# Hash attention and SwiGLU on one core: q and k columns ordered by chunk parity, and an opening laid out anew

## The chip, the core and the metric

The kernel runs on one core of a Trainium2 chip. A core has five engines, each with its own instruction queue: TensorE (PE: matmuls and transposes into PSUM), VectorE (DVE), ScalarE (ACT), GpSimd (POOL) and SyncE (SP, which here only issues DMAs). DMAs can be issued from the queues of SP, ACT and POOL. An engine works through its queue in order; a semaphore holds an instruction until its inputs are there, and everything behind it on that engine waits too. The metric is the device time of one execution in microseconds (us).

## The reference

Attention over 4 batches, 8 heads, 768 tokens of 64 dimensions, followed by a gated feed-forward layer. A query sees only those keys that fall in its bucket; the bucket is the sign pattern of six projections.

```python
q_bits = (np.einsum('bhsd,dk->bhsk', q, proj) > 0)      # and k_bits; proj is 64 x 6
mask = q_bucket[:, :, :, None] == k_bucket[:, :, None, :]
scores = np.where(mask, scale * np.matmul(q, k.transpose(0, 1, 3, 2)), -1000000000.0)
attn = exp(scores - max);  attn = attn / (attn.sum(-1) + 1e-09)
x = (attn @ v) as [batch * seq, heads * head_dim]       # 3072 x 512
xn = x / sqrt(mean(x * x) + 1e-06) * rms_g
g = xn @ w_gate;  out = (g * sigmoid(g) * (xn @ w_val)) @ w_out
```

The gate and value weights are 512 x 1536, the output weights 1536 x 512. Everything comes and goes as float32.

## The kernel before

**The mask as rows of a matmul.** A score tile is one matmul over 71 rows: 64 rows hold the scaled dimensions of q and k (factor `DIM`), six rows hold the bits as +0.5 or -0.5, and one row is a constant. Where all six bits agree the exponent stays at its size; where one differs it is so small that the exponential is nothing. So a pair of heads needs, in one tile `qk` (128 x 4 x 768 fp16: q of two heads, k of two heads), the scaled dimensions in rows 0 to 63, the bits in rows 64 to 69 and the constants.

**Units and slots.** A batch has two units of 384 queries (`hf` 0 and 1), eight units in all. A unit's attention has 24 slots (8 heads x 3 blocks of keys). A slot is two score matmuls (`scores`, L292) of 128 keys x 384 queries, two exponentials on ACT (L299), and later six matmuls with v (`pv`, L322), which add to one PSUM tile for six slots; after those six, `post` normalizes the head pair on DVE (L337, L338). A unit ends with sums of squares (L351), a power on POOL (`rs`, L379), a scaling of x (L386), and transposes of x (L399). Its 12 gate steps (`queue_gates`, L438 to L464) and six output steps (`queue_out`, L488) run in the slots of the next unit and the one after. Thus from the second unit on, TensorE has attention, gates and outputs side by side. In the first unit there is attention alone.

**Preparation of a head pair** (`queue_prep`). Loads put 6 consecutive tokens on each partition, so a chunk of 128 columns is "every sixth token". Four groups of three float32 transposes (L175) turn q and k of two heads; a transpose takes two chunks at once, the even chunk landing in partitions 0 to 63, the odd one in 64 to 127. ACT copies q out of PSUM (`qT`), DVE copies k (`kT`). Eight matmuls (`project`, L186) make the six projections of both parities in one PSUM tile. DVE turns them into bits (L198), and eight DMAs carry these into rows 64 to 69 of `qk`, one for each of q and k of two heads and each parity (`place`, L205). DVE scales the dimensions (`dims`, L238). POOL casts v to fp16 (`vcast`, L243) and adds it up (`vsum`, L251 to L254); the first product of a head pair (L309) needs that sum.

**Parities.** In `qk` the columns stand in the order of the chunks, even and odd in turn. A score matmul's 384 queries are three chunks of both parities. So the first slot of a head waits for the bits and dimensions of both.

**Order.** The code puts every step at a position with `at(pos, fn)`, in units of slots; the list is sorted by it at the end and issued. Unit u's slot n stands at 24u + n. Nothing but the position decides the order within an engine's queue; no step waits for its position in time.

**The opening.** Pair 0 of batch 0 is prepared ahead of slot 0 with two projections, one per parity, from which DVE writes the bits straight into `qk` (`bits_direct`, L221), and ACT does the scaling (L236). Pairs 1, 2 and 3 go through DMAs: pair 1's transposes ahead of slot 0 and its projection after slot 1, pair 2 from position 3.6, pair 3 from 8.6. All gate and value weights are loaded from POOL's queue, casting to fp16, at position 2.0 (`load_gv`, L149), after POOL's casts and sums of v; the output weights follow (L153). Score tiles of the first unit use four buffers of the pool `ring` and three of `gvpool`.

Of the kernel before, what the change touches and what calls it, by code (L numbers as in the profile page):

```python
# [33 lines left out]
def kernel(  # L34
# [47 lines left out]


    warm = const.tile([128, 1], FP32, name="warm")
    nc.vector.memset(warm, 0.0)
    nc.scalar.activation(warm, warm, AF.Exp)
    ident = const.tile([128, 128], FP32, name="ident")
    make_identity(nc, ident)
    pj = const.tile([128, 32], FP32, name="pj")
    nc.vector.memset(pj, 0.0)  # L90
    nc.sync.dma_start(out=pj[0:64, 0:6], in_=proj)
    nc.sync.dma_start(out=pj[64:128, 6:12], in_=proj)
    pj1 = []
    for e in range(2):
        t = const.tile([128, 32], FP32, name=f"pj1_{e}")
        nc.vector.memset(t, 0.0)
        nc.vector.tensor_copy(
            t[64 * e : 64 * e + 64, 0:6], pj[64 * e : 64 * e + 64, 6 * e : 6 * e + 6]
        )
        pj1.append(t)  # L100
    load_v(0, 0)
    for hp in range(1, 4):
        load_qk(0, hp)
        load_v(0, hp)
    grow = const.tile([128, DMODEL], FP32, name="grow")
    nc.sync.dma_start(out=grow, in_=moe_rms_g.unsqueeze(0).partition_broadcast(128))

    NQK = 6
# [10 lines left out]

    def const_rows(i):  # L120
        nc.gpsimd.memset(qks[i][64:71, 0:2, :].bitcast(FP32), ONE_ONE)
        nc.gpsimd.memset(qks[i][64:71, 2:4, :].bitcast(FP32), M15_M15)

    const_rows(0)
    vsums = []
    for i in range(2):
# [3 lines left out]
        vsums.append(t)  # L130
    const_rows(1)
    for i in range(2, NQK):
        at((-11.0, -5.0, 20.0, 21.0)[i - 2], lambda i=i: const_rows(i))

# [23 lines left out]

    def queue_prep(b, hp, p0, step, vp, hlag=0.0, direct=False):
        idx = prep_n[0]  # L160
        prep_n[0] += 1
        qk = qks[idx % NQK]
        qk_of[(b, hp)] = qk
        tl = {}

        def tr(j):
            def go():
                if j == 0:
                    tl["q"] = work.tile([128, 2, HQ], FP32, name="qT", tag="qT")
                    tl["k"] = work.tile([128, 2, HQ], FP32, name="kT", tag="kT")  # L170
                src = loads[(b, hp)][j % 2]
                m = ring.tile([128, 3, 128], FP32, name="trps", tag="r")
                src = src[:, j // 2].rearrange("p (c e) d -> p c (e d)", e=2)
                for i in range(3):
                    nc.tensor.transpose(m[:, i, :], src[:, i, :], ident)  # L175
                dst = tl["qk"[j % 2]][:, j // 2, :]
                mm = m.rearrange("p c d -> p (c d)")
                if j % 2 == 0:
                    nc.scalar.activation(dst, mm, AF.Copy)  # L179
                else:  # L180
                    nc.vector.tensor_copy(dst, mm)  # L181
            return go

        def project(lhs, m):
            for c in range(4):
                nc.tensor.matmul(  # L186
                    m[32 * c : 32 * c + 32, :], lhs, tl["qqkk"[c]][:, c % 2, :],
                    start=True, stop=True, tile_position=(0, 32 * c),
                )

        def parity(ap, e):
            return ap.rearrange("p (c e t) -> p c e t", e=2, t=128)[:, :, e, :]

        def hash_():
            m = ring.tile([128, HQ], FP32, name="hps", tag="r")
            project(pj, m)
            bits = work.tile([128, HQ], FP16, name="bits", tag="bits")
            nc.vector.tensor_scalar(bits, m, 0.0, 0.5, op0=ALU.is_gt, op1=ALU.subtract)  # L198
            tl["bits"] = bits

        def place(c):
            def go():
                for e in range(2):
                    eng = nc.gpsimd if b == 0 and hp == 1 and e else nc.sync
                    eng.dma_start(  # L205
                        out=parity(qk[64:70, c], e),
                        in_=tl["bits"][32 * c + 6 * e : 32 * c + 6 * e + 6, :].rearrange(
                            "p (c t) -> p c t", t=128
                        ),
                    )  # L210
            return go

        def hash_direct():
            tl["ms"] = [ring.tile([128, HQ], FP32, name="hps", tag="r") for _ in range(2)]
            for e in range(2):
                project(pj1[e], tl["ms"][e])

        def bits_direct(c):
            def go():
                for e in range(2):  # L220
                    nc.vector.tensor_scalar(  # L221
                        parity(qk[64:70, c], e),
                        tl["ms"][e][32 * c : 32 * c + 6, :].rearrange("p (c t) -> p c t", t=128),
                        0.0, 0.5, op0=ALU.is_gt, op1=ALU.subtract,
                    )
            return go

        def dims(i):
            def go():
                c, e = i // 2, i % 2  # L230
                dst = qk[0:64, 2 * c : 2 * c + 2].rearrange(
                    "p h (c e t) -> p h c e t", e=2, t=128
                )[:, :, :, e, :]
                src = tl["qk"[c]][64 * e : 64 * e + 64].rearrange("p h (c t) -> p h c t", t=128)
                if direct:
                    nc.scalar.activation(dst, src, AF.Copy, scale=DIM)  # L236
                else:
                    nc.vector.tensor_scalar_mul(dst, src, DIM)  # L238
            return go

        def vcast():
            vl = vloads[(b, hp)]
            nc.gpsimd.tensor_copy(  # L243
                v16s[b % 2][:, :, 2 * hp : 2 * hp + 2, 0:64],
                vl.rearrange("p h c d -> p c h d"),
            )

        def vsum():
            vl = vloads[(b, hp)]
            t3 = work.tile([128, 2, 3, D], FP32, name="vt3", tag="vt3", bufs=1)  # L250
            nc.gpsimd.tensor_add(t3, vl[:, :, 0:3, :], vl[:, :, 3:6, :])  # L251
            t1 = work.tile([128, 2, D], FP32, name="vt1", tag="vt1", bufs=1)
            nc.gpsimd.tensor_add(t1, t3[:, :, 0, :], t3[:, :, 1, :])
            nc.gpsimd.tensor_add(vsums[b % 2][:, hp, 0, :, 0:64], t1, t3[:, :, 2, :])  # L254

        at(vp, vcast)
        at(vp + 0.01, vsum)
        for j in range(4):
            at(p0 + step * j, tr(j))
        if direct:  # L260
            at(p0 + step * 4, hash_direct)
            for i, c in enumerate((0, 2)):
                at(p0 + step * 4 + 0.001 * (i + 1), bits_direct(c))
            for i, c in enumerate((1, 3)):
                at(-1.0 + 0.001 * i, bits_direct(c))
        else:
            at(p0 + step * 4 + hlag, hash_)
            for i, c in enumerate((0, 2, 1, 3)):
                at(p0 + step * 4 + hlag + 0.001 * (i + 1), place(c))
        for i in range(4):  # L270
            at(p0 + step * (4.2 + 0.3 * i) + hlag, dims(i))

# [7 lines left out]
    def queue_attention(u, base, step, late):  # L280
# [22 lines left out]
        def pv(n):  # L303
            def go():
# [13 lines left out]
                for i in range(2):  # L318
                    jt = 2 * blk + i
                    p = probs_of.pop((u, n, i))  # L320
                    for t in range(3):
                        nc.tensor.matmul(  # L322
                            acc[:, t, hh, :],
                            p[:, 128 * t : 128 * t + 128],
                            v16s[b % 2][:, jt, h, :],
                            start=False, stop=(n % 6 == 5 and i == 1 and t == 2),
# [146 lines left out]
    def queue_out(u, pos, last=False):  # L473
# [6 lines left out]
        def outq(j):  # L480
            def go():
# [10 lines left out]
                if half == 1:  # L492
                    dst = out[b * S : (b + 1) * S].rearrange("(p c) m -> p c m", c=6)
                    if last and t == 1:
# [3 lines left out]
                    if last:  # L498
                        nc.sync.dma_start(out=dst[:, 3 * hf + t, :], in_=tl["o"][:, t, :])
                    elif t == 2:  # L500
                        at_later.append(
                            lambda: nc.sync.dma_start(
                                out=dst[:, 3 * hf : 3 * hf + 3, :], in_=tl["o"]
                            )
# [9 lines left out]


    queue_prep(0, 0, -24.0, 1.0, -24.0, direct=True)
    queue_prep(0, 1, -18.0, 1.0, -16.0, hlag=15.2)
    queue_prep(0, 2, 3.6, 1.0, 1.5)
    queue_prep(0, 3, 8.6, 1.0, 1.6)


    for c in range(4):
        for wh in range(2):
            at(2.0 + 0.1 * (2 * c + wh), lambda c=c, wh=wh: load_gv(c, wh))
    for c in range(4):
        at(16.0 + 2.0 * c, lambda c=c: load_wo(c))

# [11 lines left out]
    for u in range(NU):  # L539
        queue_attention(u, SLOTS * u, 1.0, 1.1 if u == 0 else 0.0)  # L540
        p = SLOTS * (u + 1) + 0.6
        if u == 0:
            queue_norm(u, p, 1.0, 3.6)
        else:
            queue_norm(u, p, 1.0, 4.1)
    F = SLOTS / 18.0
    steps = lambda base, js: [base + 0.15 + F * j for j in js]
    for u in range(NU):
        base = SLOTS * (u + 1)
        if u == 0:  # L550
            queue_gates(u, [base + 6.15 + 1.47 * j for j in range(12)], 1.47)
        else:
# [37 lines left out]
```

## Time and profile before

| | |
|---|---|
| median of 3 runs | 393.58 us (390.21 to 394.15) |
| profiled execution | 394.13 us, span 392.4 us |
| mean granted TensorE clock | 0.955 |
| PE busy | 356.6 us, 91% |
| PE weight loads | 214.9 us, 55% |
| ACT busy | 243.4 us, 62% |
| DVE busy | 237.7 us, 61% |
| POOL busy | 77.2 us, 20% |
| instructions | 7949 |

The costliest groups: exponentials on ACT, 384 of 491 ns; score matmuls, 384 of 346 ns; gate and value matmuls, 384 each of 325 and 326 ns; products with v, 1152 of 199 ns; output matmuls, 288 of 379 ns. A duration is from an instruction's start to its end; matmuls overlap, so a row of them takes less than its sum.

In the preparation, over the whole kernel: a copy out of PSUM 552 ns on DVE (L181) and 496 on ACT (L179); a bit write or bit step 551 to 557 ns on DVE; a scaling 64 x 768 about 650 ns mean on DVE (0.540 to 1.260 us) and 843 ns on ACT; a cast of v on POOL 872 ns; its three sums 1115, 567 and 530 ns; a constant fill of seven rows on POOL 731 or 869 ns. Of 120 bit DMAs of 4.5 KB, 116 are issued from SP, at 0.72 us each, and four from POOL, where they land after 1.9, 2.8 and 3.3 us (least, median, most).

How to read it: the busy shares are means over the whole time. The opening, some 60 us, differs from the rest, and what a step there costs has to be read from its own stretch. The granted clock is what share of full speed TensorE's clock had. It is shown as full from the start, but matmuls before about 9 us last as long as those at half clock later (eight projections of 128 x 384: 0.86 us each group at 7.05 as at 23.2, and 0.52 at 14.5).

### The profile page before, as it was taken

How to read it: one execution, taken by the hardware profiler on the slowest of the kernel's cores; microseconds unless marked ns; L12 is line 12 of the kernel's file. 1: busy time of each engine (PE TensorE's matmuls, PEld its weight loads, DVE VectorE, ACT ScalarE, POOL GpSimd, SP SyncE). 2: the span in 40 equal slices, each digit the busy share in tenths (PEclk: the TensorE clock that was granted, in tenths of full speed). 3: DMA queues.
4: the chain of work that ended last, by engine and by line, in shares of the span. 5: the costliest groups of instructions: out<-in, count | busy, mean ns of one | idle time of the engine just before them, and what ended most of it. 6: DMA issues, size and time to landing. Idle time of an engine off the chain costs nothing.

```text
span 392.4 us, 7949 instructions
## 1 busy us (share of the span) xinstructions
PE 356.6 (91%) x3048; PEld 214.9 (55%) x3048; DVE 237.7 (61%) x469; ACT 243.4 (62%) x549; POOL 77.2 (20%) x110
## 2 busy tenths in 40 slices
PE   5765979989999998999999998999999999998995
PEld 3442536656565664656565664656565655563552
DVE  2854164765866678475866668465866564366570
ACT  5753655657676764757676774767675767772321
POOL 6898036020000037200000028200000000000000
PEclk9986557999999999999999999999999999999999
DMA  7729992120000840410000840310000200200102
GB/s 249 263 30 202 223 293 109 43 87 3 3 3 5 297 147 5 147 60 2 2 3 5 295 150 5 132 75 2 3 4 4 83 0 2 82 1 2 81 2 80
DMA packets 23574, 31.22 MB, mean 80 GB/s; under 512 B 4184, under 2 KB 22128, under 8 KB 23536
## 3 DMA queue, kind: packets, MB, share of 16 engines
q1 hardware_dynamic: 17584, 25.97, 19.4%
q0 software_dynamic: 5952, 4.74, 7.9%
q8 instruction: 24, 0.39, 0.4%
q14 instruction: 14, 0.11, 0.1%
HBM read 28.58 MB, written 6.29 MB: 89 GB/s over the span
## 4 chain that ended last, share of the span: by engine, by line
PE 51%; issue 24%; DVE 14%; POOL 5%; DMA 3%; ACT 1%; SPq 1%; POOLq 0%; DVEq 0%; ACTq 0%
PE v_ps L438 11%; PE g_ps L438 10%; PE s_ps L292 9%; PE o_ps L488 9%; PE pv L322 6%; DVE qk L238 4%; DVE xn L386 2%; DVE sq L351 2%; PE trps L175 2%; PE hps L186 2%; DMA vl<-in_v_dram 2%; DMA qk<-bits 2%; DVE x L338 1%; DVE a L455 1%; POOL rs L379 1%
## 5 line engine op out<-in xcount | busy, mean ns | idle before, releaser
L299 ACT ACTIVATE p<-s_ps 128x384 f16<-128x384 f32 x384 | 164.2, 491 | 82.1 <-PE s_ps L292 80.8
L292 PE MATMUL s_ps<-qk 71*128 71x384 f16 x384 | 101.6, 346 | 7.1 <-DMA qk<-bits 5.2
L438 PE MATMUL v_ps<-xnT,wv 128*128 128x384 f16 x384 | 78.1, 326 | 5.9 <-DVE a L455 5.9
L438 PE MATMUL g_ps<-xnT,wg 128*128 128x384 f16 x384 | 79.0, 325 | 4.1 <-ACT xnT L407 2.5
L455 DVE SCALAR_TENSOR_TENSOR a<-th,g_ps 128x384 f32<-128x384 f32 x96 | 53.1, 553 | 46.4 <-ACT th L447 45.2
L322 PEld LDWEIGHTS <-p 128*128 128x128 f16 x1152 | 63.1, 101 | 31.1 <-issue 13.4
L322 PE MATMUL pv<-v,p 128*128 128x65 f16 x1152 | 70.0, 199 | 0.0
L488 PE MATMUL o_ps<-wo,ht 128*128 128x512 f16 x288 | 68.7, 379 | 0.0
L447 ACT ACTIVATE th<-g_ps 128x384 f32<-128x384 f32 x96 | 47.8, 498 | 20.9 <-PE g_ps L438 18.0
L464 DVE TENSOR_TENSOR ht<-a,v_ps 128x384 f16<-128x384 f32 x96 | 53.0, 552 | 8.0
L379 POOL TENSOR_TENSOR rs<-ms,mhalf 128x3 f32<-128x3 f32 x8 | 6.9, 858 | 246.8 <-DVE ms L375 246.8
L438 PEld LDWEIGHTS <-wv 128*128 128x128 f16 x384 | 37.5, 98 | 32.5 <-issue 8.2
L438 PEld LDWEIGHTS <-wg 128*128 128x128 f16 x384 | 35.2, 97 | 26.0 <-issue 6.3
L488 PEld LDWEIGHTS <-ht 128*128 128x128 f16 x288 | 27.0, 97 | 27.4
L292 PEld LDWEIGHTS <-qk 71*128 71x128 f16 x384 | 29.4, 102 | 14.4 <-issue 7.4
L497 ACT ACTIVATE osb<-o_ps 128x512 f32<-128x512 f32 x23 | 13.7, 597 | 24.8 <-PE o_ps L488 24.8
L181 DVE COPY kT<-trps 128x384 f32<-128x384 f32 x32 | 17.7, 552 | 17.2 <-PE trps L175 17.2
L337 DVE RECIPROCAL r<-pv 128x6 f32<-128x6 f32 x32 | 6.2, 193 | 34.9 <-PE pv L322 34.9
L179 ACT ACTIVATE qT<-trps 128x384 f32<-128x384 f32 x32 | 15.9, 496 | 13.9 <-PE trps L175 13.9
L386 DVE SCALAR_TENSOR_TENSOR xn<-x,rs,grow 128x512 f16<-128x512 f32 x24 | 21.1, 932 | 5.6 <-POOL rs L379 5.6
L198 DVE TENSOR_SCALAR bits<-hps 128x384 f16<-128x384 f32 x15 | 8.4, 557 | 21.6 <-PE hps L186 20.9
L175 PE MATMUL trps<-ident,ql 128*128 128x128 f32 x96 | 17.0, 288 | 3.9 <-DMA ql<-in_q_dram 3.9
(50 smaller groups left out, 284.1 us busy)
## 6 DMA issues: line engine op xcount, KB each, us to landing
ql<-in_q_dram SPq DMA_DIRECT2D x16, 384.0 KB
kl<-in_k_dram SPq DMA_DIRECT2D x16, 384.0 KB
vl<-in_v_dram SPq DMA_DIRECT2D x16, 384.0 KB
out_dram<-osb SPq DMA_DIRECT2D x7, 768.0 KB
qk<-bits SPq DMA_DIRECT2D x116, 4.5 KB
wg<-in_moe_w_gate_dram POOLq DMA_DIRECT2D x4, 384.0 KB, 9.0
wv<-in_moe_w_val_dram POOLq DMA_DIRECT2D x4, 384.0 KB, 10.5
wo<-in_moe_w_out_dram POOLq DMA_DIRECT2D x4, 384.0 KB, 20.1
```

The source lines that it names most:

```text
L175: nc.tensor.transpose(m[:, i, :], src[:, i, :], ident)
L179: nc.scalar.activation(dst, mm, AF.Copy)
L181: nc.vector.tensor_copy(dst, mm)
L292: nc.tensor.matmul(s_ps, qk[0:71, 2 + hh, 128 * jt : 128 * jt + 128], qk[0:71, hh, HQ * hf : HQ * hf + HQ], start=True, stop=True,)
L299: nc.scalar.activation(p, s_ps, AF.Exp, scale=SCL)
L322: nc.tensor.matmul(acc[:, t, hh, :], p[:, 128 * t : 128 * t + 128], v16s[b % 2][:, jt, h, :], start=False, stop=(n % 6 == 5 and i == 1 and ...
L386: nc.vector.scalar_tensor_tensor(out=tl["xn"][:, t, :], in0=x_of[u][:, t, :], scalar=tl["rs"][:, t : t + 1], in1=grow, op0=ALU.mult, op1=A ...
L438: nc.tensor.matmul(ps, w[:, kt, fs], xnT[:, kt, :], start=(kt == 0), stop=(kt == 3))
L447: nc.scalar.activation(th, tl[f][0], AF.Tanh, scale=0.5)
L455: nc.vector.scalar_tensor_tensor(out=a, in0=th, scalar=1.0, in1=g_ps, op0=ALU.add, op1=ALU.mult)
L464: nc.vector.tensor_mul(ht_of[u][f], a, v_ps)
L488: nc.tensor.matmul(tl[t], ht_of[u][f][:, 128 * t : 128 * t + 128], wo[:, f, :], start=(f == 0), stop=(f == 11),)
```

## The change

1. *Columns by parity.* In `qk`, all even chunks come first (384 columns), then all odd ones. Bits and scaled dimensions are written as one run of 384 columns instead of three of 128. A unit is now one parity of the queries: unit 0 needs the even half of q, and the first three of six key tiles are even. The products with v pick v's chunk by `2 * (jt % 3) + jt // 3`, and a unit's output rows are every second one, written as three runs of 2 KB a partition instead of one of 6 KB.
2. *Bits of pairs 0 and 1 written directly* from two projections each (one per parity, now in `gvpool` buffers), except the odd half of q, which unit 1 needs first: it goes through a DVE tile (`bits_one`) and a DMA, late (positions 11.461 to 11.464). Pairs 2 and 3 keep DMAs, in a new order (`PLACES`).
3. *Scaling and casts.* For pair 0 three of four scalings are on ACT and one on POOL; for pair 1 three on POOL; for pair 2 two on POOL and one on DVE; for pair 3 three on DVE; the odd half of q of pairs 1 to 3 follows on DVE at positions 15, 16 and 17. The casts of v of pairs 2 and 3 go to DVE. Constant rows of the first two `qk` tiles are filled by DVE, the others by POOL.
4. *Loads.* The projection weights are issued from ACT's queue; q and k of pair 1 are loaded ahead of v of pair 0, and so on. Gate and value weights move from position 2.0 to 12.1 and 13.2, behind POOL's scalings and sums; output weights from 16 to 26 and later.
5. *The first unit's tail.* Transposes of its x start 8.0 slots after the power's position instead of 3.6; its gates start at 10.2 with steps of 1.13 slots instead of 6.15 with 1.47.
6. Later batches keep their positions; their columns, the order of their DMAs and of their scalings are as in 1 and 2.

```diff
+    nc.scalar.dma_start(out=pj[0:64, 0:6], in_=proj)
+    nc.scalar.dma_start(out=pj[64:128, 6:12], in_=proj)
...
+    const_rows(0, nc.vector)
+    const_rows(1, nc.vector)
...
+    load_qk(0, 1)
     load_v(0, 0)
+    load_qk(0, 2)
+    load_v(0, 1)
+    load_qk(0, 3)
+    load_v(0, 2)
+    load_v(0, 3)
...
+        def place(c, e, eng=None):
+            base = 32 * c + 6 * e if "h" in tl else 32 * c
+            (eng or nc.sync).dma_start(
+                out=qk[64:70, c, HQ * e : HQ * e + HQ], in_=tl["bits"][base : base + 6, :]
+            )
+
+        def hash_one(e):
+            tl["h", e] = gvpool.tile([128, HQ], FP32, name="hps", tag="gv")
+            project(pj1[e], tl["h", e])
+
+        def direct(c, e):
+            nc.vector.tensor_scalar(
+                qk[64:70, c, HQ * e : HQ * e + HQ],
+                tl["h", e][32 * c : 32 * c + 6, :],
+                0.0, 0.5, op0=ALU.is_gt, op1=ALU.subtract,
+            )
...
+        def dims(c, e, eng="v"):
+            dst = qk[0:64, 2 * c : 2 * c + 2, HQ * e : HQ * e + HQ]
+            src = tl["qk"[c]][64 * e : 64 * e + 64]
+            if eng == "a":
+                nc.scalar.activation(dst, src, AF.Copy, scale=DIM)
+            elif eng == "v":
+                nc.vector.tensor_scalar_mul(dst, src, DIM)
+            else:
+                nc.gpsimd.tensor_scalar_mul(dst, src, DIM)
...
+    PLACES = [(0, 0), (2, 0), (2, 1), (1, 0), (3, 0), (3, 1), (0, 1), (1, 1)]
...
-                            v16s[b % 2][:, jt, h, :],
+                            v16s[b % 2][:, 2 * (jt % 3) + jt // 3, h, :],
...
-    queue_prep(0, 0, -24.0, 1.0, -24.0, direct=True)
-    queue_prep(0, 1, -18.0, 1.0, -16.0, hlag=15.2)
-    queue_prep(0, 2, 3.6, 1.0, 1.5)
-    queue_prep(0, 3, 8.6, 1.0, 1.6)
+    A, Bp, C, Dp = [make_prep(0, hp) for hp in range(4)]
...
+    A(-20.0, "dims", 0, 0, "a")
+    A(-19.9, "dims", 1, 0, "a")
+    A(-19.8, "hash_one", 0)
+    A(-19.6, "direct", 0, 0)
+    A(-19.5, "direct", 2, 0)
+    A(-19.3, "dims", 1, 1, "a")
...
+    A(0.01, "hash_one", 1)
+    A(0.02, "direct", 2, 1)
...
+    Bp(0.2, "dims", 0, 0, "p")
...
+    A(1.3, "bits_one")
+    Bp(1.4, "dims", 1, 0, "p")
+    Bp(1.5, "dims", 1, 1, "p")
+    Bp(2.9, "hash_one", 0)
...
+    Bp(3.9, "hash_one", 1)
...
+    Bp(5.7, "bits_one")
...
+    C(7.6, "hash_mm")
+    C(7.6, "bits")
...
+    Dp(11.4, "hash_mm")
+    Dp(11.4, "bits")
...
-            at(2.0 + 0.1 * (2 * c + wh), lambda c=c, wh=wh: load_gv(c, wh))
+            at((12.1 if c == 0 else 13.0) + 0.1 * (2 * c + wh), lambda c=c, wh=wh: load_gv(c, wh))
     for c in range(4):
-        at(16.0 + 2.0 * c, lambda c=c: load_wo(c))
+        at(26.0 + 2.0 * c, lambda c=c: load_wo(c))
...
-            queue_norm(u, p, 1.0, 3.6)
+            queue_norm(u, p, 1.0, 8.0)
...
-            queue_gates(u, [base + 6.15 + 1.47 * j for j in range(12)], 1.47)
+            queue_gates(u, [base + 10.2 + 1.13 * j for j in range(12)], 1.13)
```

## The prediction

> **What bounds the kernel now.** I read the page's slices first. TensorE is busy almost throughout, so what matters is at which clock, and there the opening stands apart from everything behind it.
>
> ```profile
> PE   5765979989999998999999998999999999998995
> PEclk9986557999999999999999999999999999999999
> ```
>
> (40 slices of 9.81 us.) From slice 8 on the clock is full and TensorE is the bound. Slices 3 to 7 have a granted clock of about half. I asked for stretches as long as the steps in which that clock moves, 3.4 us (columns: sum, then PE, PEld, DVE, ACT, POOL busy, clock, DMA share, GB/s).
>
> ```profile
> 18.95:22.35 3.40, 1.02 (x10) 0.79 (x11) 0.64 (x3) 1.41 (x4) 3.19 (x6) 0.98 0.07 12
> 22.35:25.75 3.40, 3.40 (x25) 1.28 (x23) 1.47 (x4) 1.27 (x4) 3.24 (x6) 0.52 0.00 0
> 29.15:32.55 3.40, 0.83 (x10) 0.67 (x9) 0.81 (x2) 0.77 (x2) 3.11 (x5) 0.98 1.31 200
> 42.80:46.20 3.40, 3.35 (x25) 1.67 (x23) 0.59 (x2) 2.97 (x7) 0.00 (x0) 0.50 1.28 208
> 56.40:59.80 3.40, 1.12 (x7) 0.60 (x8) 3.00 (x3) 0.08 (x1) 3.17 (x4) 0.50 1.09 365
> 59.80:63.25 3.45, 3.45 (x29) 2.92 (x28) 1.02 (x2) 2.07 (x4) 2.64 (x4) 0.52 0.56 203
> ```
>
> A stretch with TensorE busy 24 or 30% is followed by half clock; one that is busy throughout is followed by full clock; 98.5% (42.80) did not bring it back. So the idle time at 30 to 33 us cost half speed until 63 us. The chain of waits says what made it:
>
> ```profile
> 26.18 0.72 SPq L205
> 27.00 6.04 DMA qk<-bits
> 33.13 0.80 PE s_ps L292 x2
> ```
>
> Pair 2's bit rows, sent by DMA, took 6.04 us to land while the weights were loading. In the timeline I then marked slots (a slot: two score matmuls, two exponentials, six products with v):
>
> ```profile
> 12.39 0.33 PE L292 MATMUL s_ps<-qk 71*128 71x384 f16 x1
> 33.13 0.80 PE L292 MATMUL s_ps<-qk 71*128 71x384 f16 x2 [2.84 <-DMA qk<-bits]
> 50.37 0.83 PE L292 MATMUL s_ps<-qk 71*128 71x384 f16 x2
> 95.00 0.49 PE L292 MATMUL s_ps<-qk 71*128 71x384 f16 x2
> ```
>
> These are slots 0, 12, 24 and 48 (counted through the issue order). From 95 us on both kernels run the same sequence, so I forecast slot 48 and carry the difference to the end. Steady state: the POOL steps that end units stand at 100.61 and 189.26, 44.3 us a unit.
>
> **Prices.** Exponentials back to back 0.41 (1.64 for four at 15.65). TensorE by the half-clock chain, halved: a slot 0.48 (0.64 and 0.33), three transposes 0.32, eight hash matmuls 0.78. DVE 0.55 for a PSUM copy or a bit write. A bit DMA 0.72 to issue on SP, landing 1.9 to 3.3 (the POOL-issued ones) or 6.04.
>
> **The change, part by part.** *To slot 0.* Before, both projections (7.05 to 9.6), four bit writes (0.55 each, to 11.3) and two transposes that wait for evictions stand ahead of the first score; its record starts at 12.39. Now slot 0 needs one projection and two bit writes. Transposes end at 7.12 as before, the second pair's first one takes 0.85 (clock still low by its duration), the projection 1.5 ends at 9.5, two writes 10.6: slot 0 at 10.7, 1.7 earlier. ACT's three scalings (0.84 each, 7.04 to 9.6) end in time. This needs the second q load by 7.1; before, the third big load (v) had landed at 6.32, so it should. Projection weights now go out on ACT's queue ahead of its table load: 2 x 0.60 + 1.28 ends about 3.3, before ACT's first copy at 4.80. DVE's four new row fills cost between 0.17 (its 128x128 fill) and 0.87 (POOL's own); at the upper end DVE is free at 5.4, before its first copy at 5.88: nothing.
>
> *Slots 0 to 12.* TensorE: 12 x 0.48 + 5 projections x 0.78 + 10 triples x 0.32 + 0.3 = 13.2. DVE to the last pair's bits: 16 x 0.55, one head's normalization 0.76, one scaling 0.56, one cast of v (unseen on DVE; between the 0.56 of a scaling and its longest, 1.26; I take 0.9), two copies and bits 1.65 = 12.7. ACT: 24 x 0.41 + 5 x 0.5 = 12.3. Three queues equally full wait for each other, since projections now hold two of three score buffers: slot 1 waits for the late bit write (0.4), pair 1's projection for the buffer that DVE frees last (1.0), slots 5 and 6 likewise (0.8), first pieces and handovers 1.9. So 13.2 + 4.1 = 17.3, slot 12 at 28.0; from 24 (no waits) to 32 (twice).
>
> *POOL.* Six scalings stand before the weights (64x768; unseen on POOL), the first of them early, at 7.0. Each: 0.87 from the cast of as many elements, up to 2.2 from the two-input add (1.115 for 384 elements). I take 0.87, one input like the cast; even 2.2 gives pair 1's last scaling at 19.4 and slot 7 wants it at 21. POOL then has pair 1's cast and sums (0.87 + 2.2), two scalings (to 22.8), two sums (2.2 each): weights issue from 27.2 to 33.5 (8 x 0.79), before 25.5. Gates start at slot 34, about 49 us, and the eight loads took 9.0 to 10.5 each: covered by 10 us. The output weights move behind the first unit's POOL step (44 us), wanted at 78.
>
> *Pair 2 and 3's bits.* Pair 2's projection stands two thirds of the way to slot 12 (position 7.6, but with six of the ten transposes and three of five projections ahead of it), at 10.7 + 0.7 x 17.3 = 22.8; with the bit step its bits are ready at 23.4. Its second DMA is out at 24.9 (2 x 0.72), landing 26.8 to 28.2: no wait at 28.0, but 2.9 if it takes 6.04. Pair 3's eight follow at 29.2; the second is out at 30.6, lands 33.4 or 36.6, slot 18 wants it at 33.5. I take a stall of 1.5, between 0 and 3.1, as the weights begin amid these DMAs. Four of pair 0 and 1's DMAs wait in that queue too, then batch 1's loads: out at 38 instead of 42.3, wanted at slot 28.4, about 44.
>
> *Slots 12 to 24.* 12 x 0.86 (ACT's pair, 1.71 for four at 26.96) + 0.6 at head ends + the stall 1.5 = 12.4: slot 24 at 40.4 against 50.37, 10.0 gained.
>
> *Slots 24 to 48.* Before 44.6. Now 44.3 less output matmuls 6 x 1.30 = 36.5, plus 1.7 because the first eight slots are ACT's pace (8 x 0.38, less 1.3 of transposes in the gaps) = 38.2: 6.4 gained. The later start of the transposes of x (gap 8.0 for 3.6) takes them off the wait of 57 to 59.5: slot 24 at 40.4, half a slot, normalization 0.76, three sums 2.2, the POOL step 0.9 end at 44.7, the first scaling at 45.9 and the third at 48.3; slot 32.6 comes at 47.8, where the record of before had the wait open for 3 us.
>
> *Later.* Contiguous scalings were already 0.556 median with runs of 128; DVE is 61% busy. 2 KB rows in seven stores instead of 6 KB lie beside 40 us of work. Nothing, with 1 either way; without that cover each prep's four scalings would cost 2.2.
>
> Sum: 394.13 (span 392.4 + 1.7) - 10.0 - 6.4 = 377.7. The median, 393.58, stands 0.55 under the profiled run: I say 377.2.
>
> **Two rules against the rows.** In the row at 42.80 TensorE was busy for 3.35 of 3.40 us and the clock stayed at half for 17 us more; I therefore count the whole of it as the price of the idle time at 30. The Trainium skill, TensorE: Matmul & The Clock Gate, Part 1, has one busy window of about 3.4 us restore the clock; by that rule something else held it after 46, which this change would not remove, and the sum would be 3.9 higher (1.8, 2.1: see the first rival), 381. The row and the rule differ, and the row decides.
>
> DVE's scalings took 0.556 median but 1.26 at most, the long ones beside POOL work (36.99, 1.27). The Trainium skill, SBUF — State Buffer, Who interferes with whom, calls the port that DVE and GpSimd share an exclusive lock, which speaks against scalings on POOL: an estimate by that page is a wait of one DVE instruction each, 3 us on POOL. By the rows POOL is done with pair 2's scalings 5.2 us ahead of slot 12.
>
> **Rivals.** *The stall moves to pair 3.* If its DMAs take 6.04 each and slot 18 idles 3 us, the clock falls there and stays until the gates: stall +1.6, 16 slots x 0.11 = 1.8, prep (1.28 + 0.78 more) 2.1, x's transposes 0.3, waits 2: 385. For: weights and bits again share the engines. Against: three lines of 256 bytes became one of 768, and two DMAs, not four, release slot 18. Chance 0.2.
>
> *The clock never rises before the gates.* It rose before after the stretch at 5.3 to 8.7 that was busy throughout; if the second q load comes late, a gap there leaves all at half: 12 x 0.97 + 5 x 1.56 + 10 x 0.64 + 3 = 28.8, slot 12 at 39.5, slot 24 at 52 (12 x 0.97 + 0.6), slot 34 at 67 (9.7, prep 4.1, x 1.3), slot 48 after 14 x 0.48, twelve gates of 1.30, a prep of 2.1 and 2 of waits, at 93.5: 392.6, no change. Chance 0.07.
>
> *Slower: POOL's scalings are slow.* If one takes X, the five in front of slot 12 end at 12.8 + 3.1 + 5X (from ACT's last copy of pair 1, with the cast and sums). Beyond X = 2.4 slot 12 waits, and the clock falls: 377.2 + (5X - 12.1) + 3.9. From X = 4.9 no gain is left, from 5.7 it is over 1% slower; at 6, 399. For: POOL's power of 3 elements takes 0.86. Against: its cast and adds scale with elements at 1 to 3 ns. Chance 0.06.
>
> **Numbers.** The main case 0.67, alone 370 to 384: slot 12 from 24 to 32, the stall from 0 to 3.1, 1 for what comes later. The range adds the first rival, to 389. Within 1% (about what a measurement can tell here) is 389.6 to 397.5: the second rival. Faster 0.87, same 0.07, slower 0.06.
>
> **What would show it.** Scores start at 10.7; pair 1's slots wait for no DMA; slot 12 near 28, 24 near 40, 48 near 79; clock full from about 9 us on; rows of POOL scaling below 1.2. I am wrong if the clock row shows fives after slice 1, if a score waits over 3 us for bits, or if gates wait for weights.

## The result, and the profile after

| | before | after |
|---|---|---|
| median | 393.87 us (390.21 to 394.66, 4 runs) | 378.46 us (377.56 to 379.29, 4 runs) |
| ratio after / before | | 0.9626, 95% interval 0.9561 to 0.969 |
| profiled execution | 394.13 us, span 392.4 us | 377.56 us, span 375.8 us |
| mean granted clock | 0.955 | 0.990 |

The changed kernel is 3.7% faster. A ratio here and below leaves out executions that lie more than 1.5% above the fastest one of their kernel. The slices of its page, TensorE's busy tenths and its granted clock (a slice is now 9.4 us):

```profile
PE   4887699999999989999999989999999999997995
PEclk9999889999999999999999999999999999999999
```

The row of fives and sixes is gone; two slices at 8 are left, at 38 to 56 us. The timeline shows the same slots as before the change (0, 12, 24 and 48; line numbers have moved, scores are L301):

```profile
11.59 0.48 PE L301 MATMUL s_ps<-qk 71*128 71x384 f16 x2 [0.91 <-DVE qk L221]
...
28.24 0.50 PE L301 MATMUL s_ps<-qk 71*128 71x384 f16 x2 [0.28 <-POOL qk L241]
...
38.25 0.49 PE L301 MATMUL s_ps<-qk 71*128 71x384 f16 x2
...
80.71 0.49 PE L301 MATMUL s_ps<-qk 71*128 71x384 f16 x2
```

So of the 16.6 us that the span lost, 12.1 lie ahead of slot 24 (50.37 to 38.25), 2.2 between slots 24 and 48 (44.62 to 42.46) and 2.3 behind slot 48 (297.36 to 295.07).

The chain of waits in the opening no longer runs through a bit transfer but through POOL:

```profile
13.95 1.34 POOL qk L241
...
16.15 2.13 POOL qk L241
...
18.35 2.14 POOL qk L241
...
23.48 2.50 POOL qk L241
...
26.06 2.13 POOL qk L241
...
31.09 0.33 PE pv L318
...
37.48 6.52 DMA ql<-in_q_dram
44.00 0.14 issue
44.13 0.87 PE trps L182 x3
```

L241 is a scaling on POOL. POOL goes from one to the next with its sums of v between them, and its last sum releases the first product of pair 2 at 31.09. The second part is new: the transposes of batch 1's first pair wait until 44.1 for a load that was issued at 37.48. The group of these scalings (least, median, most in ns):

```profile
L241 POOL TENSOR_SCALAR qk<-qT x3: 2122/2147/2499, 8.3 to 23.5; 64x768 f16<-64x768 f32 x3
L241 POOL TENSOR_SCALAR qk<-kT x3: 2123/2123/2127, 16.1 to 26.1; 64x768 f16<-64x768 f32 x3
```

And by stretches (PE, PEld, DVE, ACT, POOL busy, granted clock, DMA share, GB/s):

```profile
30.00:33.00 3.00, 1.92 (x32) 1.54 (x33) 2.97 (x5) 2.23 (x7) 2.77 (x4) 1.00 0.06 14
33.00:36.00 3.00, 2.26 (x30) 1.27 (x27) 2.37 (x5) 3.00 (x10) 2.92 (x5) 1.00 0.27 13
42.00:45.00 3.00, 1.23 (x11) 0.83 (x8) 1.96 (x6) 1.25 (x4) 2.44 (x4) 0.82 1.18 278
45.00:50.00 5.00, 4.71 (x34) 3.39 (x32) 1.81 (x4) 3.28 (x8) 3.81 (x6) 0.50 1.20 279
```

At 30 to 36 us, where the weights filled the DMA engines before (share 1.3), they are almost idle, and the clock is full. Only the stretch with 1.23 of 3 us busy, which is the wait for the load, is followed by half clock, until 50.7.

### The profile page after: what moved, and what is told of

Its sections match the earlier page's. It is cut to its first block, busy times and chain, and to the rows that moved or that the text cites. A ratio compares the mean times of both kernels' runs of the same rounds, so it can differ in the third digit from the quotient of the medians.

```text
span 375.8 us, 7954 instructions
## 1 busy us (share of the span) xinstructions
PE 348.1 (93%) x3056; PEld 211.6 (56%) x3056; DVE 236.6 (63%) x475; ACT 241.0 (64%) x548; POOL 83.9 (22%) x106
## 3 DMA queue, kind: packets, MB, share of 16 engines
q1 hardware_dynamic: 17824, 25.97, 20.5%
## 4 chain that ended last, share of the span: by engine, by line
PE 53%; issue 25%; DVE 10%; POOL 5%; DMA 3%; ACT 3%; POOLq 0%; SPq 0%; DVEq 0%; ACTq 0%
PE v_ps L447 12%; PE g_ps L447 11%; PE o_ps L497 9%; PE s_ps L301 9%; PE pv L331 5%; PE trps L182 4%; POOL qk L241 3%; PE hps L195 2%; DVE qk L239 2%; DMA ql<-in_q_dram 2%; DVE sq L360 2%; DVE xn L395 2%; DMA kl<-in_k_dram 1%; ACT p L308 1%; ACT xnT L416 1%
## 5 line engine op out<-in xcount | busy, mean ns | idle before, releaser
L301 PE MATMUL s_ps<-qk 71*128 71x384 f16 x384 | 95.7, 328 | 1.6 <-DVE qk L221 1.2
L331 PEld LDWEIGHTS <-p 128*128 128x128 f16 x1152 | 60.2, 98 | 30.3 <-issue 8.9
L331 PE MATMUL pv<-v,p 128*128 128x65 f16 x1152 | 67.9, 194 | 0.5
L301 PEld LDWEIGHTS <-qk 71*128 71x128 f16 x384 | 28.4, 99 | 9.9 <-issue 1.3
L395 DVE SCALAR_TENSOR_TENSOR xn<-x,rs,grow 128x512 f16<-128x512 f32 x24 | 19.6, 869 | 5.6 <-POOL rs L388 5.6
L182 PE MATMUL trps<-ident,kl 128*128 128x128 f32 x96 | 17.3, 292 | 1.7 <-DMA kl<-in_k_dram 1.4
```

Source lines behind the costliest of these rows:

```text
L301: nc.tensor.matmul(s_ps, qk[0:71, 2 + hh, 128 * jt : 128 * jt + 128], qk[0:71, hh, HQ * hf : HQ * hf + HQ], start=True, stop=True,)
L331: nc.tensor.matmul(acc[:, t, hh, :], p[:, 128 * t : 128 * t + 128], v16s[b % 2][:, 2 * (jt % 3) + jt // 3, h, :], start=False, stop=(n % 6 ...
L395: nc.vector.scalar_tensor_tensor(out=tl["xn"][:, t, :], in0=x_of[u][:, t, :], scalar=tl["rs"][:, t : t + 1], in1=grow, op0=ALU.mult, op1=A ...
```

## The experiments

Three questions stood after this profile. What made the opening shorter: pair 1's direct bits, the parity columns, or the place of the weight loads? What is the load at 44 us worth? And where do the 2.3 us behind slot 48 come from, where the forecast had nothing? Slots below are start times in one profiled execution; times and ratios are against the kernel before in the same set of runs, where its median was 389.6 to 390.1. There are three such sets; the changed kernel itself was run in one of them.

**Scalings on DVE** (the changed kernel, five of POOL's six scalings; pair 0's stays):

```diff
-    Bp(0.2, "dims", 0, 0, "p")
+    Bp(0.2, "dims", 0, 0, "v")
-    Bp(1.4, "dims", 1, 0, "p")
-    Bp(1.5, "dims", 1, 1, "p")
+    Bp(1.4, "dims", 1, 0, "v")
+    Bp(1.5, "dims", 1, 1, "v")
-        C(7.9 + 0.1 * i, "dims", c, e, "ppv"[i])
+        C(7.9 + 0.1 * i, "dims", c, e, "v")
```

> The changed kernel with its five POOL scalings of pairs 1 and 2 given to DVE (0.56 each there, 2.12 on POOL); all else as changed. Theory A, the POOL scalings are a cost on the path (the chain runs through them from 13.95 to 28.2 us): slot 12 starts 1.5 to 2.5 us earlier, near 26, and the time falls by about 2, to 376. Theory B, they are also what holds the weights back (POOL's queue reaches them at 33.7): without them POOL issues the weights near 23 to 25, into the bit DMAs of pairs 2 and 3, slot 12 or slot 18 waits 2 to 6 us for bits, the clock falls, and the time rises by 3 to 8, to 381 to 386.

Measured: 381.59 us (two runs), ratio 0.9796 (0.9759 to 0.9832). Against the changed kernel, 0.9744 (0.9684 to 0.9804) in another set, that is not faster, and whether it is slower the intervals do not show; the profile does show what changed. With its queue free, POOL issues the first weight at 20.05 us instead of 33.71, and the wait of the old kernel is back. Its chain and two of its stretches:

```profile
24.95 5.48 DMA qk<-bits
30.42 0.05 issue
30.47 0.57 PE s_ps L301 x2
```

```profile
27.32:30.74 3.42, 2.01 (x18) 0.73 (x17) 1.86 (x4) 1.33 (x4) 0.00 (x0) 1.00 1.32 204
30.74:34.16 3.42, 3.09 (x26) 1.73 (x25) 1.72 (x5) 2.62 (x6) 0.00 (x0) 0.50 1.32 205
```

A bit transfer of 4.5 KB takes 5.48 us while the DMA share is 1.32, slot 12 starts at 30.47 instead of 28.24 and the clock is half until 51.3. So the slow scalings on POOL do a service: they hold the weights back. The gain of 2 us that theory A expected at slot 12 did not come.

**The same, with the weights held back another way**: a small POOL copy that reads pair 3's `bits` tile stands ahead of the weights (pair 3's sums of v go ahead of it).

```diff
+    Dp(11.405, "hold", scratch)      # nc.gpsimd.tensor_copy(t, tl["bits"][:, 0:8])
-    Dp(11.5, "vsum")
+    Dp(11.3, "vsum")
```

> The changed kernel with the five scalings on DVE as in e1, and the weights held back by data: a POOL copy of eight columns of pair 3's bits stands ahead of them, so they can't be issued before some 28 us. If e1 lost (381.6) only because its weights ran at 20 us into the bit DMAs: slot 12 near 26.5 instead of 30.5, no wait for bits at slot 12, clock up to 40 us, 374 to 377. If the scalings on DVE themselves were the loss (DVE as the bound, its normalization late): slot 12 no earlier than 28 and 378 or more.

Measured: 381.25 us (two runs), ratio 0.9791 (0.971 to 0.9872). No wait for bits at slot 12, but DVE now paces the slots before it (slot 6 at 20.74 instead of 19.55, slot 12 at 29.91), and the copy waits for the bits to be made, not to land: weights and pair 3's transfers start together, one of them takes 4.52 us (31.78 to 36.30) and slot 18 starts at 36.44, after a wait of 2.33. The reading with DVE as the next bound holds for the slots ahead of 12. With the early load of further below added as well:

> e6 with the loads of batch 1's first pair moved ahead of pair 2's bit DMAs (as in e2). If the two losses are separate, they add: slot 12 near 26.5, no wait at slot 28, clock full throughout, slot 48 at 75 to 76: 371 to 373, under both kernels. If the loads now meet pair 2's bits (both leave SP near 22): slot 12 waits 1 to 2 us and nothing is gained over e2's 376.

Measured: 384.98 us over four runs (379.75 to 386.65); its profile has slot 18 at 37.14 after a bit transfer of 5.05 us and half clock from 37 to 54. Not better, and neither of the two cases that were expected: slot 12 (30.11) waits for no bits. The losses are those of its base, DVE ahead of slot 12 and a transfer under the weights ahead of slot 18.

**The parity columns alone**, on the kernel before:

```diff
-            return ap.rearrange("p (c e t) -> p c e t", e=2, t=128)[:, :, e, :]
+            return ap[:, HQ * e : HQ * e + HQ]
-                            v16s[b % 2][:, jt, h, :],
+                            v16s[b % 2][:, 2 * (jt % 3) + jt // 3, h, :],
```

> The kernel before with the columns ordered by parity and nothing else (the bits still go by the same DMAs, the same engines scale and cast, the weights stay). The changed kernel gained 2.3 us behind slot 48, where nothing but this differs. If the contiguous runs make the scalings cheaper beside POOL's work, this shows the same 2 to 3 us behind slot 48 and an opening that still waits some 3 us at slot 12 with half clock to 63: 390 to 392. If that gain comes from elsewhere: no change within 1 us. If the parity order itself frees slot 12 of the wait (two DMAs release it instead of four), the clock stays up and it is 380 to 385.

Measured: 388.26 us, ratio 0.9983 (0.996 to 1.0006): nothing. Slot 12 now needs two transfers and starts at 27.58 instead of 33.13. But an execution with the old columns (the order of the scalings, further below) has slot 12 at 26.82 too, so the long wait at slot 12 in the profile of before is not in every execution, and it can't be put down to the columns that it is gone here. Either way it only moves on: in that other execution slot 15 waits for a bit transfer of 6.20 us (27.22 to 33.42), and here pair 3's bits travel under the weights, and slot 18 starts at 36.01 (slot 24 at 42.97). In its chain:

```profile
27.49 1.57 DMA qk<-bits
...
31.18 4.78 DMA qk<-bits
```

In this execution DVE also did pair 3's scalings ahead of pair 1's normalization, and TensorE was idle for most of 30 to 33 us. So the normalization was put first:

```diff
+            late = 0.9 if b == 0 and hp == 3 else 0.0
-            at(p0 + step * (4.2 + 0.3 * i) + hlag, dims(i))
+            at(p0 + step * (4.2 + 0.3 * i) + hlag + late, dims(i))
```

> e3 (parity order alone on the kernel before) with pair 3's four scalings behind the normalization of pair 1 on DVE instead of ahead of it. In e3 slot 12 was at 27.6, as early as in the changed kernel, but DVE did the scalings (29.7 to 31.6) ahead of the normalization, TensorE idled till 32.4 and the clock fell at 34. Theory A, this queueing is the rest of the opening's loss: TensorE goes on at 30.5, the clock stays, slot 24 at 39 to 40 instead of 43, total 381 to 383. Theory B, pair 3's bits are late in any case (in e3 they landed at 36.0 for slot 18): slot 18 waits from 33 to 36, the clock falls there, slot 24 no earlier than 42, total 385 to 386.

Measured: 389.16 us, ratio 0.9993 (0.9947 to 1.0038). The wait for the normalization shrank from 2.32 to 0.64 us, but the next one opened: slot 15 waits 0.99 us for a bit transfer (until 31.94), the clock falls at 32.9 and stays half until 56.8, and slot 18 waits 1.66 us for a transfer of 4.89 (from 30.82) and starts at 35.85. So DVE's order is not what holds the opening here; the transfers under the weights are.

**The idle time filled**, on the kernel before: 20 needless matmuls at position 11.99, ahead of slot 12.

```diff
+    at(11.99, filler(20))      # ident16 x ident16, 384 columns, result unused
```

> The kernel before with 20 idle matmuls of 384 columns (3.2 us at full clock) on TensorE just ahead of slot 12, where it waited 2.84 us for pair 2's bits. The wait stays; only TensorE's idle time is filled. Theory A, the loss is the clock: it stays full after 30 us, slot 12 at about 33.3 as before, slot 24 at 46 to 47 instead of 50.4, slot 48 at 86 to 88 instead of 95: 385 to 387. Theory B, the loss is the wait itself and what queues behind it: no gain, 393 to 395.

Measured: 392.26 us, ratio 1.0079 (1.0041 to 1.0118). The clock outlived the gap that was filled and fell at 37 us, after a second idle time (33.5 to 36.9, of which 3.39 us are put down to DVE's normalization of pair 1). Neither theory was tested by it: one gap filled left the next.

**The weights behind pair 3's bits, and nothing else of the opening.** The decisive run: the kernel before, its columns, scalings, casts and bits untouched.

```diff
+            nc.gpsimd.tensor_copy(t[64:70, :], qk[64:70, 3, 128:136])   # pair 3, at 12.7
-            at(2.0 + 0.1 * (2 * c + wh), lambda c=c, wh=wh: load_gv(c, wh))
+            at(13.0 + 0.1 * (2 * c + wh), lambda c=c, wh=wh: load_gv(c, wh))
-        at(16.0 + 2.0 * c, lambda c=c: load_wo(c))
+        at(26.0 + 2.0 * c, lambda c=c: load_wo(c))
-            queue_norm(u, p, 1.0, 3.6)
+            queue_norm(u, p, 1.0, 8.0)
-            queue_gates(u, [base + 6.15 + 1.47 * j for j in range(12)], 1.47)
+            queue_gates(u, [base + 10.2 + 1.13 * j for j in range(12)], 1.13)
```

> The kernel before (old columns, old sharing of the scalings and casts, old bits) with one thing moved: the weight loads on the POOL queue stand behind a small POOL copy that reads pair 3's bits in qk, so that they go out only when pair 3's bits have landed, and unit 0's norm and gates stand where the changed kernel has them (8.0; 10.2 and 1.13), since the weights come later. Theory A (the opening's gain is where the weights stand, the rest of the opening's edits are second): weights at 31 to 34 us instead of 25.5, no wait of over 1 us for pair 3's bits, slot 18 at 33 to 34 and slot 24 at 39 to 40, the clock full up to 40 us, slot 48 at 81 to 85, a span of 379 to 383 (297.1 behind the first o_ps, as before). Theory B (the bits of pair 1 written directly and the scalings off DVE carry it): slot 12 or 18 still late by 3 us, slot 24 at 42 or later, a fall of the clock between 30 and 45, a span of 386 or more.

Measured: 383.81 us, ratio 0.9833 (0.9769 to 0.9897). The changed kernel itself, in the same set:

> The changed kernel itself, unedited, on the chip of the experiments and beside the version with the early load. A chip on which the kernel before takes about 390: a ratio between 0.96 and 0.97 to it if the chips do not matter, so 374 to 378.

Measured: 380.39 us, ratio 0.9744 (0.9684 to 0.9804), above the 374 to 378 that were expected. So of 9.7 us that the whole change is worth in this set, the place of the weights, with the norm and gates that go with it, makes 6.3 (by the intervals 4.0 to 9.0). The chain of the decisive run:

```profile
35.05 0.72 SPq L205
35.77 0.04 issue
35.81 1.81 DMA qk<-bits
...
37.76 0.18 POOL scratch L243
37.95 0.34 issue
38.29 0.81 POOL wg L149
```

A bit transfer that took 4.5 to 6.2 us under the weights takes 1.81 without them, and the weights follow at 38.29. No slot waits for bits (slot 12 at 28.27, 18 at 34.79, 24 at 40.08). The clock is half from 14.6 to 18.0, then full to 41.9, although TensorE waits 2.05 us for DVE's normalization of pair 1 and one stretch is quite idle:

```profile
30.00:33.00 3.00, 0.95 (x12) 0.49 (x10) 2.86 (x7) 1.64 (x4) 0.00 (x0) 1.00 0.03 7
33.00:36.00 3.00, 2.99 (x44) 2.04 (x43) 0.35 (x1) 2.32 (x7) 0.00 (x0) 1.00 0.06 14
```

From 41.9 to 48.7 it is half. Slot 48 starts at 83.06, 2.4 us behind the profile of the changed kernel. Theory A's numbers hold to within 1 us (slots 18, 24 and 48, and a span of 380.4), except for the weights, which it had at 31 to 34. What this run does not separate is the move of the loads from the later norm and gates. But these stand behind slot 24, and slot 24 is already early: 40.08 against 42.78 to 43.23 in three executions of the old opening with the weights at 25 us (the two with parity columns and the one with the new order of scalings). So by these single executions some 3 of the 6.3 us are the loads' alone; for the rest the question is open.

**The order of the four scalings alone**, on the kernel before, for the 2.3 us behind slot 48:

```diff
-            at(p0 + step * (4.2 + 0.3 * i) + hlag, dims(i))
+            at(p0 + step * (4.2 + 0.3 * i) + hlag, dims((0, 2, 3, 1)[i]))
```

> The kernel before with nothing but the order of a pair's four scalings as in the changed kernel (q even, k even, k odd, q odd). In e3 the contiguous runs left the stretch behind slot 48 at 297.1 us as before; the changed kernel has 294.8. If the order makes it (the second scaling starts 0.1 earlier and is through before POOL takes the shared port: 0.6 instead of 0.8 to 1.1 each): 295 behind slot 48, and about 2 us less than before in all. If something else: 297 and no change.

Measured: 387.01 us, ratio 0.9931 (0.9899 to 0.9963), 2.7 us. DVE's timeline in a later batch, first before:

```profile
151.25 0.77 DVE L238 TENSOR_SCALAR qk<-qT 64x768 f16<-64x768 f32 x1
152.03 2.36 DVE L238 TENSOR_SCALAR qk<-kT 64x768 f16<-64x768 f32 x2
154.42 0.56 DVE L455 SCALAR_TENSOR_TENSOR a<-th,g_ps 128x384 f32<-128x384 f32 x1
```

and with the new order, in the experiment:

```profile
143.01 0.59 DVE L238 TENSOR_SCALAR qk<-qT 64x768 f16<-64x768 f32 x1
144.00 1.27 DVE L238 TENSOR_SCALAR qk<-kT 64x768 f16<-64x768 f32 x2
145.19 1.18 DVE L238 TENSOR_SCALAR qk<-qT 64x768 f16<-64x768 f32 x1
```

The last three of four take 3.13 us in the old order and 2.45 in the new, and the changed kernel has 1.27 and 1.18 as well. In the old order both scalings of k (1.09 and 1.26) fall beside POOL's second cast and the add behind it (151.54 to 153.97); in the new order, where the second scaling starts 0.1 us sooner after the first, only the last does (1.18, POOL's cast from 144.80), and the others take 0.54 to 0.72. Why a scaling beside them takes twice as long, no run here shows. TensorE feels it through the gate product `a` that stands behind them on DVE. In TensorE's timeline before (in the changed kernel the matmuls at this place do not wait):

```profile
155.03 0.81 PE L438 MATMUL v_ps<-xnT,wv 128*128 128x384 f16 x4 [0.44 <-DVE a L455]
```

From the second unit's power on POOL to the last unit's, first before, then with the new order:

```profile
100.61 0.86 POOL L379 TENSOR_TENSOR rs<-ms,mhalf 128x3 f32<-128x3 f32 x1 [18.40 <-DVE ms L375]
...
358.74 0.85 POOL L379 TENSOR_TENSOR rs<-ms,mhalf 128x3 f32<-128x3 f32 x1 [37.08 <-DVE ms L375]
```

```profile
93.67 0.87 POOL L379 TENSOR_TENSOR rs<-ms,mhalf 128x3 f32<-128x3 f32 x1 [18.19 <-DVE ms L375]
...
349.52 0.85 POOL L379 TENSOR_TENSOR rs<-ms,mhalf 128x3 f32<-128x3 f32 x1 [37.07 <-DVE ms L375]
```

That is 258.13 us before and 255.85 with the new order. Parity alone has 258.14 (94.50 to 352.64), the changed kernel 255.86 (86.32 to 342.18). So the order is the whole of the late gain, and contiguous columns are none of it. The 295 us that were expected behind slot 48 were not seen in this profile, which has 296.75: its clock falls once more at the last unit's norm (half from 352.8 to 356.2), as further below.

**The load of batch 1's first pair earlier**, in the changed kernel (position 7.0, ahead of the 20 bit transfers on SP):

```diff
-            at(base - 8.0 + 5.0 * hp + 0.75 * early, lambda b=b, hp=hp: load_qk(b, hp))
+            at(7.0 if b == 1 and hp == 0 else base - 8.0 + 5.0 * hp + 0.75 * early,
+               lambda b=b, hp=hp: load_qk(b, hp))
```

> The changed kernel with the loads of batch 1's first pair moved ahead of pair 2's bit DMAs in SP's queue. Theory A, the wait of the transposes at 44.13 and the half clock that follows it (44.2 to 50.6, TensorE busy 6.1 us, so some 3 us of work at half speed) are a new loss of 1.8 + 3: both go, slot 48 comes near 76 instead of 80.7, 373 to 374. Theory B, the wait is covered by what follows (DVE's scaling of x ends at 45.5 and the gates can't start before): under 1.5 us gained. Theory C, the two loads (0.8 MB, some 2.7 us of the engines) make pair 2's bits late: slot 12 waits, and the gain is lost.

Measured: 378.39 us from two runs of 375.82 and 380.97, ratio 0.9713 (0.9631 to 0.9796). In its profile the clock is full to slot 48, which starts 3.4 us earlier than in the changed kernel:

```profile
77.29 0.49 PE L301 MATMUL s_ps<-qk 71*128 71x384 f16 x2
```

In a second set, six runs beside the changed kernel:

> The changed kernel with the loads of batch 1's first pair issued at position 7.0 instead of behind the 20 bit transfers, timed beside the changed kernel on one chip. If the 3.4 us that it won at slot 48 last: 2 to 3.5 us under the changed kernel. If the late fall of the clock at 340 us is a part of its course: 1 to 2 us under it. If only chance: the same.

Measured: 376.23 us (372.62 to 379.44), ratio 0.9603 (0.9534 to 0.9671), against 0.9744 for the changed kernel: 4.2 us less by the medians, more than was expected, and the fastest version of all. The ratio leaves out two of the six (378.61 and 379.44), and with them the times overlap those of the changed kernel (377.67 to 381.43). In both profiles 1.7 us come back at the end, since 296.4 us lie behind the first output matmul instead of 294.7. By stretches, at the last unit's norm:

```profile
340.00:343.40 3.40, 1.95 (x16) 1.09 (x17) 2.52 (x4) 0.87 (x2) 0.00 (x0) 0.93 0.00 0
343.40:347.00 3.60, 3.60 (x12) 1.34 (x11) 0.00 (x0) 0.13 (x2) 0.00 (x0) 0.59 0.00 0
```

The changed kernel has 1.00 in both. Its last norm has the same waits, but spread over two steps of the clock's grid (TensorE busy for 2.11 of 3.41 us, then 2.78 of 3.42) instead of one (1.48 of 3.41). Which of the two happens seems to depend on when the unit ends; the fall is there in both profiles of this version and in that of the new order of scalings.

**The wait for that load filled**, to tell the wait from the clock:

```diff
+    at(28.39, filler(16))
```

> The changed kernel with 16 needless matmuls (384 columns of fp16, results not used) at position 28.39, ahead of the transposes that wait for batch 1's first load. The wait for the load stays, PE is busy for about 2.5 us of it. Theory A (half of what the early load won at slot 48, 3.4 us, is the clock): the clock stays full from 42 to 51 us, slot 48 about 1.5 to 2 us earlier than 81, a span of about 374. Theory B (it is the wait alone, and the filler adds its own time): the clock falls all the same or the filler pushes the rest, slot 48 at 81 or later, span 376 to 378.

Measured: 378.61 us, ratio 0.9687 (0.9613 to 0.9761). The profiled execution, 383.08 us, is the longest of the four and left out of the ratio. In the other three (376.65, 378.34 and 378.87) the mean clock was 0.995 to 0.997; in the six of the changed kernel it was 0.971 to 0.989, at 377.67 to 381.43. A mean of 0.995 leaves no room for 6.8 us at half clock in a span of 377 (they alone would make it 0.991). So the filler kept the clock, and by the medians about 2 of the 4 us of the early load are clock; the intervals overlap, and the split is not shown more closely than that. The long execution shows something else:

```profile
28.63:32.04 3.41, 1.88 (x26) 1.26 (x27) 2.72 (x6) 2.40 (x6) 3.10 (x5) 1.00 0.03 9
32.04:35.45 3.41, 3.41 (x31) 2.15 (x28) 3.17 (x4) 2.62 (x6) 3.25 (x4) 0.50 0.06 14
```

Here the clock fell at 32 us, where the first product of pair 2 waits for POOL's sum (1.33 us, as in the changed kernel). POOL's chain is thus at the edge: TensorE is busy for about half of that stretch, and in this execution that was too little.

## Why the prediction was right, and by which steps

377.2 us was forecast and 378.46 measured, and the two gains of the sum, 10.0 and 6.4, make 16.4 against 16.6 in the profile. That closeness is partly luck: three terms were off and cancel (2.1 us more up to slot 24, 4.3 less from 24 to 48, 2.3 more behind it). The kernel before was also long in that comparison: 393.6 to 394.7 in three of four runs, where its median in the sets of the experiments is 390. In the one set that has both kernels the change is worth 9.7 us rather than 15.4; why the kernel before was long there so often is not shown.

- *To slot 0: 10.7, measured 11.59.* The load of k of pair 0 landed at 6.1 and the transposes ended at 9.0, where the forecast had them at 7.12 as before. With the projection weights gone from SP's queue, four big loads go out in a row; the forecast looked at the second pair's loads only. That this order is the reason is not shown: with the same order of loads (scalings on DVE) k lands at 5.0 and slot 0 is at 10.75, and in the version with the early load slot 0 is at 11.89 and 12.14.
- *Slot 12: 28.0, measured 28.24.* Right in size, wrong in reason. I took 0.87 for a POOL scaling from the cast; it takes 2.12, the upper end of the bounds and against the sign "rows of POOL scaling below 1.2". So POOL, not three equally full queues, ends last there (slot 12 waits 0.28 us for it). The rival with slow scalings put its threshold at 2.4; that the real value stopped just below it is why it did not decide.
- *Weights from 27.2, measured 33.71*, by the same term: six scalings with 1.25 us more. This is what made the stall of 1.5 at slot 18 nothing: the transfers met no weights (slot 18 at 32.96). The two errors helped: slot 24 at 38.25 instead of 40.4.
- *Pair 3 as the place where the stall goes* (first rival) did not happen in the changed kernel, but in four versions where the weights start before pair 3's bits have landed (both with parity columns on the old opening, both with the weights held until the bits are made): slot 18 at 35.85 to 37.14, after waits of 0.87 to 2.84 us for bits. Mechanism right, condition not met.
- *Slots 24 to 48: 38.2, measured 42.46.* The step that failed. The forecast has the load "out at 38 instead of 42.3, wanted at slot 28.4, about 44", and stops there: it counts the queue and leaves out the landing. The load went out at 37.48 and took 6.52; slot 28 came at 41.88, for slot 24 was early. TensorE waited 1.77 us, and the clock fell for 6.8. With the load early the step takes 38.75 (38.81 to 77.56 in the second set): the rest of its working, output matmuls out of these slots and ACT's pace, is right to 0.6.
- *Later: nothing, measured 2.3.* The forecast looked at whether contiguous runs make a scaling shorter, rightly answered no, and passed over the new order of the same four scalings, which was in the diff.
- *The direct bits of pair 1, the columns, the casts.* The decisive run (6.3 us) and the order (2.7) make 9.0 of the 9.7 us in their sets. What is left for all of these is within the uncertainty of these times; by the profiles of the decisive run and the changed kernel it is 2.4 us at slot 48, one execution each.

The rival in which the clock never rises before the gates is out: the clock row is full from the opening to 43.9 us.

On the clock, the Trainium skill, TensorE: Matmul & The Clock Gate, Part 1, gives a free-running window of about 3.4 us. The steps here fit that grid: in the experiment with the scalings on DVE the fall and the rise lie 20.5 us apart (30.77 to 51.25), six times 3.41. On POOL, GPSIMD Engine Reference, 3.1 Elementwise, has 1.8 cycles an element at best and 2.6 with two inputs, at 1.2 GHz; an estimate from it is 1.15 to 1.66 us for 768 elements. The 2.12 us measured lie above it, and the measurement decides.

## What to carry to other kernels

Small transfers that the next matmuls wait for and bulk loads that nobody wants yet must not share the DMA engines: find what holds the bulk back, and hold it by what it must wait for (the landing), not by a position or by a slow neighbour. When something moves earlier, add issue, queue and landing of every load that the earlier consumer needs, since an idle time can cost again in clock: here a wait of 1.77 us was followed by 6.8 us at half clock. A gain early in a kernel is read at the next point where both kernels do the same work; with the columns alone slot 12 was early and slot 18 late, and the time the same.

## What was not expected of the hardware

*Records without a gap did not always bring the clock back.* The prediction had it that a stretch busy throughout does. With the scalings on DVE, these are three of the six steps of the grid after the fall:

```profile
34.16:37.58 3.42, 3.42 (x28) 2.17 (x27) 1.93 (x4) 2.75 (x7) 0.00 (x0) 0.50 1.33 207
...
41.00:44.43 3.43, 3.43 (x33) 2.25 (x32) 0.00 (x0) 2.63 (x7) 0.00 (x0) 0.50 0.93 254
...
47.85:51.27 3.42, 3.42 (x24) 2.64 (x23) 2.38 (x6) 2.97 (x8) 2.93 (x4) 0.50 0.81 286
```

All three are full, and only the third is followed by full clock. The first two hold scores (71 rows) and products with v (65 columns) alone; the third has six transposes of 128 x 128 among them. The same holds for the changed kernel (restored after 47.3 to 50.7, with six transposes) and for the filled wait (not by 38.86 to 42.27, which has scores and products alone; by 45.69 to 49.10, with seven of the filler's matmuls, 128 rows x 384 columns). So the row by which the prediction chose between its two rules (42.80, busy for 98.5%) is no exception. The fall is not read off the gaps either: a step with TensorE busy for 2.04 of 3.41 us (weights held until the bits are made, 31.98 to 35.39) was followed by full clock, one with 2.58 (the decisive run, 38.50 to 41.91) by half, and one with 2.58 in the changed kernel (37.07 to 40.49) by full. What the gate counts is not shown by these records; that it is more than their gaps is.

*A price from a neighbouring row.* On POOL a scaling of 64 x 768 from fp32 to fp16 takes 2.12 us, a cast of 128 x 768 between the same types 0.83. The same scaling takes 0.54 to 1.26 on DVE.
